# The last row tile's output in column pieces of 512, 64 and 64, the first two stored together

**Chip, cores, metric.** One core of a Trainium2 chip. The metric is the device time of one execution in microseconds (us), the median of several runs. The trace's span, from first to last instruction, is some 1.8 us shorter than that time.

## The reference

```python
xn = layernorm(x)                                   # x: 2048 x 640, bf16
s = attention(xn @ wq, k_cache, v_cache) @ wo       # 32 heads of 192, 2048 keys; wo: 6144 x 640
g = silu(silu_glu(xn, w1, w3, w2))                  # gated feed-forward, 2048 x 640
return x + s * g
```

## The kernel before

Attention (about 1640 us) is followed by the rest of the feed-forward and then by the output stage. That stage takes the 16 row tiles of 128 rows one by one: 48 matmuls for each column piece (the contraction of 6144 in slices of 128), a VectorE multiply by 0.5 and the gate, a VectorE add of x, and a store issued by ScalarE. All tiles but the last use pieces of 384 and 256 columns and one store. The last tile has pieces of its own.

```python
def _output_stage(nc, i, oT, g, wo_sb, x2, out2, sb, ps_pools, last=False):
    D = out2.shape[1]                                # 640; P = 128
    OC = wo_sb.shape[1]                              # 48
    cuts = [(0, D - P), (D - P, D)] if last and D - P <= 512 else _column_pieces(D)
    # ... xt (rows of x), tmp (fp32) and res (bf16) are 128 x 640
    for b, (c0, c1) in enumerate(cuts):
        w = c1 - c0
        ps = ps_pools[b % len(ps_pools)].tile([P, 1024], F32, tag="st2", name="ps_s")
        for k in range(OC):
            nc.tensor.matmul(ps[:, 0:w], lhsT=oT[:, k, :], rhs=wo_sb[:, k, c0:c1], start=(k == 0), stop=(k == OC - 1))
        nc.vector.scalar_tensor_tensor(out=tmp[:, c0:c1]..., in0=ps[:, 0:w]..., scalar=0.5,
                                       in1=g[:, c0 // P:c1 // P, :], op0=ALU.mult, op1=ALU.mult)
        nc.vector.tensor_tensor(out=res[:, c0:c1], in0=tmp[:, c0:c1], in1=xt[:, c0:c1], op=ALU.add)
        if last:
            nc.scalar.dma_start(out=_tile_rows(out2, i)[:, c0:c1], in_=res[:, c0:c1])
    if not last:
        nc.scalar.dma_start(out=_tile_rows(out2, i), in_=res[:])
# ... after the loop over the row tiles:
good = nc.values_load(flag[0:1, 0:1], ...)           # every engine loads the flag into a register
with tc.If(good < 2 * P):                            # and branches over a long block that these
    _exact_attention(...)                            # inputs never take
```

After its last instruction each engine loads the flag and jumps over the exact-attention block to the end of its program.

## Time and profile before

| | before |
|---|---|
| median time, 6 runs | 1938.13 us (1937.98 to 1938.29) |
| span of the profiled run | 1936.43 us |
| start of the last 512-column matmul | 1928.17 us |
| **tail**: from there to the end of the span | 8.25 us |

The change can reach nothing but the tail, so the tail is what I compare in all traces. It does not contain what the first 1928 us do from run to run. Times written with a plus sign (+3.42) are counted from the start of that last 512-column matmul and come, as all times to the nanosecond here, from the single records of the trace. A group line reads: line, engine, operation, output and inputs, shapes, count, then busy us and mean ns of one, then idle time in front and its cause. A line of waits reads: who waited, for whom, us in total, times, longest us. A q behind an engine's name (PEldq is TensorE's, SPq is SyncE's) marks what is no computation: branches, semaphores, DMA issues. The prediction shows the lines themselves.

### The profile page before, as it was taken

How to read it: one execution, taken by the hardware profiler on the slowest of the kernel's cores; microseconds unless marked ns; L12 is line 12 of the kernel's file. 1: busy time of each engine (PE TensorE's matmuls, PEld its weight loads, DVE VectorE, ACT ScalarE, POOL GpSimd, SP SyncE). 2: the span in 40 equal slices, each digit the busy share in tenths (PEclk: the TensorE clock that was granted, in tenths of full speed). 3: DMA queues.
4: the chain of work that ended last, by engine and by line, in shares of the span. 5: the costliest groups of instructions: out<-in, count | busy, mean ns of one | idle time of the engine just before them, and what ended most of it. 6: DMA issues, size and time to landing. Idle time of an engine off the chain costs nothing.

```text
span 1936.4 us, 59669 instructions
## 1 busy us (share of the span) xinstructions
PE 1926.6 (99%) x27273; PEld 1315.6 (68%) x27281; DVE 654.6 (34%) x997; ACT 1180.0 (61%) x1279; POOL 282.5 (15%) x501
## 2 busy tenths in 40 slices
PE   9999999999999999999999999999999999999998
PEld 6666666666666666666666666666666666577776
DVE  7333333333333333333333333333333334521111
ACT  6677676767676767776777777677767677210000
POOL 3111111111111111111111111111111110000000
PEclk9999999999999999999999999999999999999999
DMA  8643433323333434363434343434334220937783
GB/s 181 129 101 67 98 68 86 84 62 88 59 90 61 100 63 97 68 162 69 101 66 100 69 101 69 101 64 101 69 69 96 58 68 2 260 69 137 151 152 62
DMA packets 394643, 178.98 MB, mean 92 GB/s; under 512 B 341616, under 2 KB 382832, under 8 KB 394384
## 3 DMA queue, kind: packets, MB, share of 16 engines
q1 hardware_dynamic: 371136, 125.32, 31.6%
q0 software_dynamic: 19472, 45.71, 10.0%
q8 instruction: 215, 3.52, 0.8%
q10 hardware_dynamic: 3776, 4.06, 0.7%
q14 instruction: 44, 0.36, 0.1%
HBM read 52.82 MB, written 27.79 MB: 42 GB/s over the span
## 4 chain that ended last, share of the span: by engine, by line
PE 99%; DVE 1%; DMA 0%; ACT 0%; issue 0%; DVEq 0%; ACTq 0%
PE obank L519 35%; PE st L487 34%; PE ps L424 14%; PE ps_s L111 11%; PE ps_f L731 3%; PE ps_gu L705 1%; PE st L488 1%; PE ps L410 0%; DVE stats L316 0%; DMA x_all<-in_A_x_dram 0%; PE ps L391 0%; PE pst L354 0%; PE pk L271 0%; DVE xn L346 0%; ACT pT L493 0%
## 5 line engine op out<-in xcount | busy, mean ns | idle before, releaser
L493 ACT ACTIVATE pT<-st 128x1024 bf16<-128x1024 f32 (+1 forms) x1025 | 1046.1, 1021 | 250.2 <-PE st L488 234.0
L519 PEld LDWEIGHTS <-pT 64*128 64x128 bf16 x16384 | 711.3, 94 | 242.3 <-ACT pT L493 0.6
L519 PE MATMUL obank<-vt,pT 64*128 64x193 bf16 x16384 | 849.7, 243 | 0.0
L487 PE MATMUL st<-qC,KW 64*128 64x512 bf16 x2046 | 605.6, 376 | 0.1
L528 DVE COPY osum<-obank 128x772 f32<-128x772 f32 x128 | 123.1, 962 | 787.1 <-PE obank L519 787.1
L488 PE MATMUL st<-qB,KW 64*128 64x512 bf16 x1024 | 385.0, 376 | 0.0
L487 PE MATMUL st<-qA,KW 64*128 64x512 bf16 x1022 | 384.3, 376 | 0.1
L488 PE MATMUL st<-qC,KW 64*128 64x512 bf16 x1022 | 384.3, 376 | 0.0
L488 PE MATMUL st<-qA,KW 64*128 64x512 bf16 x1022 | 384.3, 376 | 0.0
L487 PEld LDWEIGHTS <-KW 64*128 64x128 bf16 x3068 | 278.5, 94 | 153.7 <-issue 2.1
L424 PE MATMUL ps<-xnT,W 64*128 64x512 bf16 x1280 | 297.2, 376 | 0.0
L424 PE MATMUL ps<-xnS,W 64*128 64x512 bf16 x1280 | 296.0, 376 | 0.0
L488 PEld LDWEIGHTS <-KW 64*128 64x128 bf16 x3068 | 278.5, 94 | 0.5
L377 POOL DMA_DIRECT2D qC<-qA x124 | 65.4, 528 | 1283.0 <-DVE rl_all L535 1268.2
L430 ACT CAST qB<-ps 128x512 bf16<-128x512 f32 x131 | 76.7, 585 | 228.2 <-PE ps L424 222.6
L111 PE MATMUL ps_s<-wo_sb,oT 128*128 128x384 bf16 (+3 forms) x1535 | 208.8, 299 | 0.1
L424 PEld LDWEIGHTS <-W 64*128 64x128 bf16 x2560 | 122.9, 94 | 121.4 <-issue 0.2
L111 PEld LDWEIGHTS <-oT 128*128 128x128 bf16 x1536 | 148.4, 98 | 60.4
L529 DVE TENSOR_TENSOR osum<-osum,obank 128x772 f32<-128x772 f32 x128 | 122.7, 959 | 13.4
L536 DVE TENSOR_TENSOR ostage<-osum,rl_all 128x768 bf16<-128x768 f32 x128 | 122.7, 958 | 6.3 <-DMA o_scr<-ostage 1.9
L465 DVE SCALAR_TENSOR_TENSOR hT<-pt,qB 64x512 bf16<-64x512 bf16 x64 | 43.8, 684 | 197.4 <-ACT pt L464 197.4
L429 DVE CAST qA<-ps 128x512 bf16<-128x512 f32 x131 | 90.6, 692 | 25.3 <-PE ps L410 7.2
(84 smaller groups left out, 621.9 us busy)
## 6 DMA issues: line engine op xcount, KB each, us to landing
o_scr<-ostage SPq DMA_DIRECT2D x16, 1536.0 KB, 10.6
vt<-in_A_v_cache_dram SPq DMA_DIRECT2D x63, 384.0 KB, 5.9
qC<-qA POOLq DMA_DIRECT2D x248, 64.0 KB, 1.9
qC<-qB POOLq DMA_DIRECT2D x124, 64.0 KB, 2.3
wo_sb<-in_A_wo_dram POOLq DMA_DIRECT2D x1, 7680.0 KB, 36.1
W<-in_A_wq_dram POOLq DMA_DIRECT2D x32, 160.0 KB, 3.6
W<-in_B_w_dram POOLq DMA_DIRECT2D x32, 80.0 KB, 3.3
W<-in_A_wq_dram POOLq DMA_DIRECT2D x32, 80.0 KB, 3.0
```

The costliest lines, as they stand in the source:

```text
L111: nc.tensor.matmul(ps[:, 0:w], lhsT=oT[:, k, :], rhs=wo_sb[:, k, c0:c1], start=(k == 0), stop=(k == OC - 1))
L377: nc.gpsimd.dma_start(out=qC[0:64, half, :], in_=qAB[half][64:P, :])
L424: nc.tensor.matmul(ps[:, r * 512:(r + 1) * 512], lhsT=W[rows, j, :], rhs=xs[rows, j // 2, qs], start=(j == 0), stop=(j == 2 * DC - 1))
L429: a = nc.vector.tensor_copy(out=qAB[0][:], in_=ps[:, 0:512])
L430: b = nc.scalar.copy(out=qAB[1][:], in_=ps[:, 512:1024])
L487: nc.tensor.matmul(st2[:, 0:512], lhsT=ka, rhs=qa, start=r == 0 and nr == 3, stop=r == nr - 1)
L488: nc.tensor.matmul(st2[:, 512:1024], lhsT=kb, rhs=qb2, start=r == 0 and nr == 3, stop=r == nr - 1)
L493: nc.scalar.activation(out=pT2[:, c * w:(c + 1) * w], in_=st2[:, c * w:(c + 1) * w], func=ACT.Exp, scale=att_scale)
L519: nc.tensor.matmul(obanks[r][:, j * 256:j * 256 + DH + 1], lhsT=pT2[r * 64:(r + 1) * 64, t * 512 + j * P:t * 512 + (j + 1) * P], rhs=vt[r ...
L528: nc.vector.tensor_copy(out=osum[:], in_=ov[0])
L529: nc.vector.tensor_tensor(out=osum[:], in0=osum[:], in1=ov[1], op=ALU.add)
L536: nc.vector.tensor_tensor(out=ostage[:, qb * 4:qb * 4 + 4, hg * DH:(hg + 1) * DH], in0=osum[:, :, 0:DH], in1=rl.unsqueeze(2).to_broadcast( ...
```

## The change

Intent: shorten what follows the last matmul. The last piece shrinks from 128 to 64 columns, so that its two VectorE instructions and its store are smaller; the middle piece is stored with the first, so there are still two stores.

```diff
-    cuts = [(0, D - P), (D - P, D)] if last and D - P <= 512 else _column_pieces(D)
+    cuts = [(0, D - P), (D - P, D - 64), (D - 64, D)] if last and D - P <= 512 else _column_pieces(D)
...
+        wa = min(w, P)
         nc.vector.scalar_tensor_tensor(...                       # the same, in groups of wa columns
-        if last:
-            nc.scalar.dma_start(out=_tile_rows(out2, i)[:, c0:c1], in_=res[:, c0:c1])
+        if last and b > 0:
+            d0 = c0 if b > 1 else 0
+            nc.scalar.dma_start(out=_tile_rows(out2, i)[:, d0:c1], in_=res[:, d0:c1])
```

More of the change, by code (lines that the diff above doesn't have):

```diff
@@ L111, in _output_stage @@
             nc.tensor.matmul(ps[:, 0:w], lhsT=oT[:, k, :], rhs=wo_sb[:, k, c0:c1], start=(k == 0), stop=(k == OC - 1))
-        nc.vector.scalar_tensor_tensor(out=tmp[:, c0:c1].rearrange("p (a w) -> p a w", w=P),
-                                       in0=ps[:, 0:w].rearrange("p (a w) -> p a w", w=P),
-                                       scalar=0.5, in1=g[:, c0 // P:c1 // P, :], op0=ALU.mult, op1=ALU.mult)
+        wa = min(w, P)
+        nc.vector.scalar_tensor_tensor(out=tmp[:, c0:c1].rearrange("p (a w) -> p a w", w=wa),
+                                       in0=ps[:, 0:w].rearrange("p (a w) -> p a w", w=wa),
+                                       scalar=0.5, in1=g[:, c0 // P:-(-c1 // P), c0 % P:c0 % P + wa], op0=ALU.mult, op1=ALU.mult)
         nc.vector.tensor_tensor(out=res[:, c0:c1], in0=tmp[:, c0:c1], in1=xt[:, c0:c1], op=ALU.add)
-        if last:
-            nc.scalar.dma_start(out=_tile_rows(out2, i)[:, c0:c1], in_=res[:, c0:c1])
+        if last and b > 0:
+            d0 = c0 if b > 1 else 0
+            nc.scalar.dma_start(out=_tile_rows(out2, i)[:, d0:c1], in_=res[:, d0:c1])
     if not last:
```

## The prediction

Two terms of its sum lose their source by this: the 29.2 ns for a pair of 64 columns and the 27 ns by which such a matmul's stream is shorter. The sum came to +0.06 us: the last matmul starts 0.150 later, less 0.027 makes +0.123 for the start of the last multiply (1931.394), less 0.067 for the smaller multiply makes +0.056 for the last add and all that follows it; 1938.26 + 0.06 = 1938.32. An estimate from the trace of before comes to the same two figures: the 512-column matmuls of the last tile start 215.82 ns apart (1918.462 to 1928.174, 45 steps) and those of 128 columns 55.83, so 64 columns are 26.67 ns, and a pair of 64 columns takes 55.83 - 26.67 = 29.16 ns. In the 3.03 us after VectorE's branch the records have two packets of 8,192 bytes on an instruction queue, starting at 1933.25 and 1933.94. That VectorE waited for them was my reading.

> **What bounds the kernel now.** I read the head of the page first, then the chain of work that ended last, then the trace's last 10 us, because the change touches only the sixteenth and last row tile of the output stage.
>
> ```profile
> span 1936.4 us, 59669 instructions
> PE 1926.6 (99%) x27273; PEld 1315.6 (68%) x27281; DVE 654.6 (34%) x997; ACT 1180.0 (61%) x1279; POOL 282.5 (15%) x501
> PE 99%; DVE 1%; DMA 0%; ACT 0%; issue 0%; DVEq 0%; ACTq 0%
> ```
>
> TensorE is busy for 99% of the span, and the chain is 99% TensorE. All of that except the last few microseconds is the same code before and after. The change can therefore move only the tail, and 2% of 1938 us is 39 us, twice the 18 us that lie between the last tile's first matmul (about 1918.05) and the end of the span.
>
> The same chain in order of time, cut to the end:
>
> ```profile
> 1918.46 12.79 PE ps_s L111 x94
> 1931.25 0.02 issue
> 1931.27 0.30 DVE tmp L112
> 1931.57 0.02 issue
> 1931.60 0.29 DVE res L115
> ```
>
> The reader is to see that after the last matmul come two VectorE instructions (multiply by the gate, add x) and then nothing that the view shows until 1936.4: 4.5 us of ending. The groups of instructions within the output stage give sizes:
>
> ```profile
> L111 PE MATMUL ps_s<-wo_sb,oT 128*128 128x512 bf16 x47 | 10.5, 379 | 0.1
> L111 PE MATMUL ps_s<-wo_sb,oT 128*128 128x128 bf16 x48 | 2.8, 219 | 0.0
> L112 DVE SCALAR_TENSOR_TENSOR tmp<-ps_s,hT 128x512 f32<-128x512 f32 x1 | 0.7, 692 | 9.5 <-PE ps_s L111 9.5
> L112 DVE SCALAR_TENSOR_TENSOR tmp<-ps_s,hT 128x128 f32<-128x128 f32 x1 | 0.3, 292 | 1.3 <-PE ps_s L111 1.3
> L115 DVE TENSOR_TENSOR res<-tmp,xt 128x128 bf16<-128x128 f32 x1 | 0.3, 292 | 0.0
> ```
>
> What lies in the last 4.5 us? The waits of the queue on SyncE in the last 12 us, and the records of the exit branch and of the closing semaphores by engine:
>
> ```profile
> SPq L806 <- DVEq L754: 1.0, 1, 1.0
> ```
>
> ```profile
> L754 PEldq COMPARE_BRANCH  x1: 3395/3395/3395, 1930.7 to 1930.7; - x1
> L754 DVEq COMPARE_BRANCH  x1: 72/72/72, 1932.2 to 1932.2; - x1
> L754 PEldq EVENT_SEMAPHORE  x1: 51/51/51, 1934.1 to 1934.1; - x1
> L754 DVEq EVENT_SEMAPHORE  x1: 21/21/21, 1935.3 to 1935.3; - x1
> ```
>
> SyncE closes the program. It has seen the last store land at 1933.74 (record of its semaphore), works through a row of checks until 1934.375, and then waits 1.007 us for VectorE. VectorE starts its last add at 1931.597, its load of the flag (line 752) at 1931.612, its branch over the exact-attention block at 1932.228, and signals only at 1935.330, 3.03 us after the branch ended. From there to the end of the span are 1.10 us. So **the end hangs on when VectorE reaches its branch, not on the store**: the store has about 1.0 us of slack.
>
> [...] the 48 matmuls of 128 columns start 55.8 ns apart (1928.390 to 1931.014 in the records, over 47 steps), each with its own weight load. [...] One place in the trace shows more, the two-column matmul of the flag count:
>
> ```profile
> 1686.44 0.10 PEld L742 LDWEIGHTS <-ones 128*128 128x128 bf16 x1
> 1686.55 0.17 PE L742 MATMUL cnt<-okb,ones 128*128 128x2 bf16 x1
> 1686.55 0.12 PEld L731 LDWEIGHTS <-hT 128*128 128x128 bf16 x2
> 1686.57 0.32 PE L731 MATMUL ps_f<-w_all,hT 128*128 128x384 bf16 x1
> ```
>
> To the nanosecond the records read 1686.545, 1686.546 and 1686.573: the full weight load that followed the narrow matmul held the next one back by only 28 ns. [...]
>
> **The change part by part.** Instruction order: VectorE gets two instructions more (one more multiply and add), TensorE 96 more (48 weight loads, 48 matmuls), ScalarE still issues two stores, and no new wait appears on the PSUM buffer of the third piece (the first pool's other buffer, last used one tile earlier).
> 1. TensorE. Removed: 48 matmuls of 128 columns at 55.8 ns. Added: 96 of 64 columns. [...] First narrow matmul at 1928.390 as now, last at 1928.390 + 95 x 0.0292 = 1931.164, against 1931.014: +0.150. [...] Today the multiply starts 0.257 after the last matmul's start; then 0.230: 1931.394.
> 2. VectorE, last piece. By the slope (692-292)/384 = 1.04 ns a column, 64 columns cost 292 - 67 = 225 ns. Add starts 0.225 + 0.034 (the present gap: 1931.597-1931.271-0.292) after 1931.394, at 1931.653: **+0.056** against now. It ends at 1931.878, against 1931.889: -0.011.
> 3. VectorE, middle piece. Its matmuls end about 1929.8 + 0.2, while the 512-column add runs until 1930.010; two instructions of 225 ns then finish at about 1930.53, 0.87 us before the last piece needs the engine. Hidden.
> 4. Stores. The first moves from 1930.04 to about 1930.56 and grows from 128 to 144 KB. At the 1.7 us to landing that the DMA view has for the present one, it lands about 1932.3. The second shrinks from 32 to 16 KB and is issued 0.01 earlier; its landing time is nearly all fixed (1.8 us for 32 KB, 1.7 for 128 KB). ScalarE is free long before. Both stay under the 1.0 us of slack: worth nothing.
> 5. Ending. The flag load started 15 ns after the start of the last add, so it follows the add's start, +0.056, and the branch, the fetch and the close follow in fixed steps. Sum: +0.06 us, or -0.01 if it is the add's end that counts.
>
> **The rivals.**
> - *The weight load becomes TensorE's bound.* At 40 ns a pair the last matmul would start 0.0400 x 95 = 3.80 us after the first instead of 2.62: +1.2 us, about 1939.4; at today's 55.8 ns it would be +2.7, about 1940.9. For it: weight loads are recorded at 98 ns each, and no sustained stretch of narrow pairs exists in this trace. Against: the 28 ns case, and the attention's 16,384 pairs, 35% of the span, at some 41 ns each [...].
> - *The store sets the end.* Then the smaller last store would gain a little: its 256-byte packets took 18 ns and would take somewhat less; at best 0.1 us, about 1938.2. Against: SyncE's 1.007 us of waiting for VectorE after the store landed.
> - *The fetch after the branch changes.* [...] one more or one fewer fetch is worth about 0.7 us (the distance of the two 8,192-byte packets), either way. TensorE's branch also comes later: its flag load ran 0.93 us, about 17 pairs, before its last matmul, so with pairs of 29.2 ns it comes at about 1930.68 instead of 1930.09, and its signal at 1934.73 instead of 1934.13, still 0.6 us before VectorE's.
>
> **Range and chances.** The middle case gives 1938.26 + 0.06 = 1938.32. The three runs before spread over 0.3 us, so low 1937.7; rivals mostly lengthen, so high 1939.5, which takes in a 40 ns pair and one fetch more. I put 1938.4, a tenth of microsecond up for that skew. A move of 39 us is out of reach for any of these: 0.5% each for faster and slower.
>
> **What would show it.** Right: the 96 narrow matmuls start about 29 ns apart and the last at 1931.15 to 1931.2; VectorE's last two instructions take about 225 ns; SyncE still waits longest for VectorE at the close; the second store lands near 1933.7. Wrong: narrow pairs at 40 ns or more; SyncE waiting for a store or for TensorE; a different stretch between VectorE's branch and its signal; or any difference before 1918 us larger than that at the tail.

## The result, and the profile after

The changed kernel took 1938.58 us, median of six runs (1938.0 to 1939.49), against 1938.13 for six of the kernel before. The ratio is 1.0003, 95% interval 0.999 to 1.0016: the same. (A ratio is the mean time of one kernel's fast runs over that of the other's of the same rounds, so not quite the ratio of the medians.)

The profiled run of the changed kernel is the slowest of its six, with a span 1.30 us longer. The two traces split this cleanly: 1.04 us was lost before the last 512-column matmul and 0.255 us in the tail.

The 1.04 us is no part of the change: it was lost in the first head. The waits of the changed kernel between 10 and 27 us have a line that the kernel before does not have:

```profile
PE ps L426 <- DMA xnS<-xnT: 0.9, 1, 0.9
```

TensorE waited 0.9 us for a copy that landed at 20.18 us, against 19.01 before. (A further 0.09 us is the first load of x.) Two more traces of the changed kernel below have no such wait.

The tail is what concerns us. The groups of the last two tiles in the changed kernel, and the last steps of its chain of work in order of time (start, length, what):

```profile
L111 PE MATMUL ps_s<-wo_sb,oT 128*128 128x64 bf16 x96 | 3.0, 193 | 0.0
L113 DVE SCALAR_TENSOR_TENSOR tmp<-ps_s,hT 128x64 f32<-128x64 f32 x2 | 0.5, 225 | 0.9 <-PE ps_s L111 0.9
L116 DVE TENSOR_TENSOR res<-tmp,xt 128x64 bf16<-128x64 f32 x2 | 0.4, 224 | 0.1
```

```profile
1919.50 12.90 PE ps_s L111 x142
1932.41 0.02 issue
1932.43 0.24 DVE tmp L113
1932.67 0.02 issue
1932.69 0.22 DVE res L116
```

The reader sees what was forecast: 96 narrow matmuls in much the time that 48 wider ones took (12.90 us for the tile instead of 12.79), and VectorE instructions of 225 ns instead of 292. Counted from the last 512-column matmul, the last matmul starts at +2.985 instead of +2.840, the last add at +3.475 instead of +3.423, and the last store is issued at +3.732 instead of +3.747.

What was not forecast stands in the DMA view of the last 10 us (KB, then us from issue to the landing of the store's last part). Before:

```profile
out_dram<-res ACTq DMA_DIRECT2D x1, 128.0 KB, 1.7
out_dram<-res ACTq DMA_DIRECT2D x1, 32.0 KB, 1.8
```

After:

```profile
out_dram<-res ACTq DMA_DIRECT2D x1, 144.0 KB, 1.7
out_dram<-res ACTq DMA_DIRECT2D x1, 16.0 KB, 3.1
```

The last store was halved, and it took 3.1 us instead of 1.8. The waits of SyncE's queue at the close show the consequence. Its first line holds the waits for the two stores: the longest is for the first, the rest is for the last (12.3 - 10.3 = 2.0 us before, 13.3 - 10.6 = 2.7 us after). Before:

```profile
SPq L754 <- SPq L754: 12.3, 2, 10.3
```

After:

```profile
SPq L756 <- SPq L756: 13.3, 2, 10.6
SPq L808 <- PEq L808: 0.7, 2, 0.5
```

The wait of 1.0 us for VectorE that the prediction shows for the kernel before is gone. VectorE's signal did come a little earlier (+7.028 instead of +7.156), but that is not why: SyncE itself came later, because it first waited for the store until +6.804 instead of +5.570.

Packet by packet: the store's 128 packets of 128 bytes are all read by +4.80, except for eight, which start from +5.542 on. Eight of 128 would be the share of one of the 16 DMA engines that the page counts, and the landings agree: the store signals in 16 parts, of which 15 have landed by +5.157 and the last lands at +6.787. (In the kernel before 15 have landed by +5.207 and the last lands at +5.554, so there too one part is late, by much less.) While the eight wait, a fetch of 16,384 bytes of instructions runs from +4.670 to +5.562: it is the one that follows TensorE's exit branch at +3.106. In the kernel before that branch came at +2.507, its fetch ran from +3.471 to +4.359, and it was over when the last store's packets started. The records of branch and signal in the changed kernel (count, then min/median/max ns, then first and last start):

```profile
L756 PEldq COMPARE_BRANCH  x1: 4112/4112/4112, 1932.3 to 1932.3; - x1
L756 DVEq COMPARE_BRANCH  x1: 72/72/72, 1933.3 to 1933.3; - x1
L756 DVEq EVENT_SEMAPHORE  x1: 21/21/21, 1936.2 to 1936.2; - x1
L756 PEldq EVENT_SEMAPHORE  x1: 51/51/51, 1936.5 to 1936.5; - x1
```

**Theory (collision).** The narrow pieces let TensorE reach its exit branch 0.60 us later. The fetch behind the branch then occupies one DMA engine just when the last store is due, and that engine's share of the store lands late. (Waiting for the fetch is not the whole delay: the eight packets are read 0.96 us after the others, but their part lands 1.63 us after the other 15. The remaining 0.67 us is not explained.) **Rivals.** The 128-byte rows or the narrow pieces make the store late by themselves; joining the stores does it; or all of it is run-to-run chance.

### The profile page after: what moved, and what is told of

Same layout as the page of the kernel before. It is cut to its first block, busy times and chain, and to the rows that moved or that the text cites. A ratio compares the mean times of both kernels' runs of the same rounds, so it can differ in the third digit from the quotient of the medians.

```text
span 1937.7 us, 59767 instructions
## 1 busy us (share of the span) xinstructions
PE 1927.8 (99%) x27321; PEld 1316.7 (68%) x27329; DVE 654.5 (34%) x999; ACT 1181.1 (61%) x1279; POOL 282.4 (15%) x501
## 4 chain that ended last, share of the span: by engine, by line
PE 98%; DMA 1%; DVE 0%; ACT 0%; issue 0%; DVEq 0%; ACTq 0%; SPq 0%
PE obank L521 35%; PE st L489 33%; PE ps L426 14%; PE ps_s L111 11%; PE ps_f L733 3%; PE ps_gu L707 1%; PE st L490 1%; DMA xnS<-xnT 0%; PE ps L412 0%; DVE stats L318 0%; DMA x_all<-in_A_x_dram 0%; ACT KW L279 0%; PE pst L356 0%; ACT xnT L358 0%; DVE xn L348 0%
## 5 line engine op out<-in xcount | busy, mean ns | idle before, releaser
L111 PE MATMUL ps_s<-wo_sb,oT 128*128 128x256 bf16 (+3 forms) x1583 | 208.9, 295 | 0.1
```

## The experiments

Kernels are compared only within the same rounds. Every result was correct. The tails decide.

**1. The kernel before, again.** No edit.

> The kernel before, unchanged, timed against itself: the yardstick. I call tail the time from the start of the last 512-column matmul of the last row tile to the end of the span; the first profile of before has 8.25 us, of the changed kernel 8.51. Theory (chance at the start): the 1.04 us by which the changed kernel's profile was late already at 26 us comes from how late a load of the first head lands and has nothing to do with the change, so runs of this same kernel will also now and then be about 1 us longer: within ten runs at least one of 1938.8 us or more. Rival (the change makes the start slow): all runs of this kernel stay within 1937.9 to 1938.4. Tail: 8.2 to 8.3 us, SyncE waiting longest for VectorE.

Median 1938.19 us (1937.99 to 1938.41, 5 runs), against 1938.40 for the nine runs of the same kernel beside it (ratio 0.9999, 0.9985 to 1.0013). Tail 8.251 us, SyncE waiting 0.8 us for VectorE. The tail repeats to a nanosecond. Neither forecast on the start held here: the longest of the 14 runs took 1938.70. In the third call, though, six of the nine runs of the kernel before took more than 1938.6 us and three over 1939.3. So runs 1 us longer do occur with the old code; that these few share the late copy of the first trace was not seen, as they left no trace.

**2. The changed kernel, again,** and **12. a third time.** No edit.

> The changed kernel, unchanged. Theory (chance at the start): median within 0.5 us of the kernel before of the same rounds, some runs at 1938.0 to 1938.2 and some about 1 us longer; tail about 8.3 us (predicted +0.06) if no packet of the last store lands late, up to 8.5 if one does as in the first profile. Rival (the change makes it slower): every run at least 0.3 us over the runs before, tail again 8.5. The 96 narrow matmuls 29 ns apart in either case.

> The changed kernel a third time, for the spread of its tail. Theory (collision): TensorE's fetch starts between 4.0 and 4.9 us, eight of the last store's packets start only when it ends, the last landing follows some 1.1 to 1.3 us after the fetch's end, at 6.3 to 6.9 us, and the tail is 8.35 to 8.6 us; median time 0.1 to 0.5 us over the kernel before of the same rounds.

Medians 1938.59 (against 1938.40 beside it; ratio 1.0002, 0.9988 to 1.0016) and 1938.57 (against 1938.85; ratio 0.9999, 0.9985 to 1.0013): the sign of the difference itself turns round. So the third call's forecast of a median 0.1 to 0.5 us over the kernel before failed (it is 0.28 under), and in the call of the second trace no run came at 1938.0 to 1938.2, where some were expected (they took 1938.33 to 1939.16). Tails 8.400 and 8.383 us, so all three traces of the changed kernel are longer than both of the kernel before, by 0.13 to 0.26 us. In all three the eight packets start when TensorE's fetch ends: fetch until +5.261 and packets from +5.248, fetch until +5.413 and packets from +5.399. The stores' landings in the DMA view, second and third trace:

```profile
out_dram<-res ACTq DMA_DIRECT2D x1, 16.0 KB, 2.7
```

```profile
out_dram<-res ACTq DMA_DIRECT2D x1, 16.0 KB, 2.9
```

The narrow matmuls are 29 ns apart (median; 30 at most) in each.

**3. The join undone.**

```diff
-        if last and b > 0:
-            d0 = c0 if b > 1 else 0
-            ...store columns d0:c1
+        if last:
+            ...store columns c0:c1
```

> The changed kernel with its join undone: pieces of 512, 64 and 64, each stored by itself as soon as it is done. If joining the first two stores matters (rival: the later and larger first store collides with the last one and makes its last packet land late), the last store lands here at about 1.45 us after its issue in all packets and the tail falls to 8.3. If it does not (theory: landing of the first store has slack either way), the tail is that of the changed kernel within 0.1 us, and the stray late packet comes or stays away by chance.

Median 1939.04 us (1938.92 to 1939.39) against 1938.40; tail 9.120 us: worse than either expectation. The store collides as in the changed kernel (fetch +4.712 to +5.588, last landing +6.861), so the join is not what makes it late. But SyncE goes on from that landing to the end in 2.24 us, not 1.70. SyncE meets this landing first, with all its other closing checks still to come: its waits show one piece of 35.2 us, where the changed kernel has two of 13.3 us together (that the third store's semaphore stands first in SyncE's row is how I read it):

```profile
SPq L755 <- SPq L755: 35.2, 1, 35.2
```

Joining the first two stores is therefore worth some 0.5 us against three stores (2.24 - 1.70, one trace each), and not by the transfer: the last landing is only 0.07 us later (+6.861 against +6.787).

**4. One store.** The kernel before, pieces 512 and 128, a single store of all 640 columns at the end.

```diff
-        if last:
-            nc.scalar.dma_start(...[:, c0:c1]...)
-    if not last:
-        nc.scalar.dma_start(out=_tile_rows(out2, i), in_=res[:])
+    nc.scalar.dma_start(out=_tile_rows(out2, i), in_=res[:])
```

> The kernel before with pieces of 512 and 128 but a single store of all 640 columns after the second. VectorE and TensorE do what they did. Theory (the end hangs on VectorE's exit branch, the store has 1 us of slack): 160 KB instead of 32 KB after the last add lands about 0.2 to 0.4 us later, inside the slack, and the tail stays 8.2 to 8.35. Rival (the store sets the end): the tail grows by 0.2 us or more.

Median 1938.22 (against 1938.40), last landing +5.670 for 160 KB, inside the slack as the theory said, though not the 0.2 to 0.4 us later that it expected: the two traces of before have +5.554 and +5.742. Tail 8.067 us, a little under the range: VectorE needed 2.92 us from its branch to its signal, against 3.10 in both traces of before. That stretch varies from 2.92 to 3.24 us over the traces of kernels with the branch.

**5. TensorE late in the kernel before.** This is the test of the theory: pieces, VectorE and stores as before, and only TensorE's branch later.

```diff
+    if last:
+        pd = ps_pools[0].tile([P, 1024], F32, tag="st2", name="ps_d")
+        for k in range(12):
+            nc.tensor.matmul(pd[:, 0:P], lhsT=oT[:, k, :], rhs=wo_sb[:, k, 0:P], start=(k == 0), stop=(k == 11))
```

> The kernel before (pieces 512 and 128, two stores), with twelve more 128-column matmuls at TensorE's very end whose result nobody reads, so that TensorE reaches its exit branch about 0.6 us later (as the changed kernel's does) while VectorE, the pieces and the stores stay as they were. Theory (collision): the fetch of instructions that follows TensorE's branch now starts at 4.1 to 4.7 us after the last 512-column matmul instead of 3.47, eight of the last store's 128 packets wait until it is over, the last landing moves from 5.55 to 5.75 us to 6.3 to 6.9 us, and the tail grows from 8.25 to 8.35 to 8.6 us. Rival (the late packets come from 128-byte rows or from the narrow pieces themselves): last landing stays at most 5.8 us and the tail stays 8.25 us.

TensorE's branch came at +3.224, its fetch ran from +4.824 to +5.724, eight of the 256-byte packets started from +5.698 on, and the last landing was at +6.893. The DMA view:

```profile
out_dram<-res ACTq DMA_DIRECT2D x1, 128.0 KB, 1.7
out_dram<-res ACTq DMA_DIRECT2D x1, 32.0 KB, 3.1
```

The same 32 KB that land in 1.8 us in the kernel before take 3.1. Tail 8.612 us; median 1938.47 against 1938.22 (ratio 1.0000, 0.9987 to 1.0014). The start of the fetch and the tail lie a little above the ranges expected (4.7 and 8.6). The late landing needs neither narrow pieces nor 128-byte rows; a late branch on TensorE is enough, in this one trace. (The twelve matmuls also make TensorE's program longer; no run separates that from the later branch.) Nor do the narrower rows add much to it: from the end of TensorE's fetch to the last landing are 1.17 us here, with 256-byte rows, and 1.20 to 1.25 us in the three traces of the changed kernel.

**6 and 7. The flag loaded early,** in the kernel before and in the changed one.

```diff
     for i in range(NQT):
+        if i == NQT - 1:
+            good = nc.values_load(flag[0:1, 0:1], ...)
         ...
-    good = nc.values_load(flag[0:1, 0:1], ...)
     with tc.If(good < 2 * P):
```

> The kernel before with the flag for the exit branch loaded into each engine's register ahead of the last row tile instead of behind it; the branch stays where it was. Theory (the end hangs on VectorE's branch): the branch comes 0.62 us earlier on VectorE, directly after the start of the last add, and the tail falls from 8.25 to about 7.65 us, the time to about 0.6 us under the kernel before; TensorE's fetch starts before 3 us. Rival (the store sets the end): tail falls by 0.2 us at most.

> The same earlier flag load in the changed kernel. Theory (collision of TensorE's fetch with the last store): TensorE's branch comes at about 2.5 us again as in the kernel before, its fetch is over at about 4.4 us, before the last store's packets at 4.7; the last store lands by 5.8 us, not 6.5 to 6.8, and the tail is about 7.7 us, 0 to 0.1 us over the same edit of the kernel before. Rival (the narrow pieces cost the 0.2 us themselves): it stays 0.15 to 0.25 us above the same edit of the kernel before.

Before with the edit: VectorE branches at +3.435 instead of +4.054, tail 7.601 us, as expected. This is the version that the experiments point to; its tail beats both kernels by 0.65 us or more. Its time does not show that: median 1938.05 (1937.43 to 1939.06) against 1938.22, ratio 1.0000, 0.9987 to 1.0014.

Changed kernel with the edit: tail 7.850 us and last landing +6.131, not 7.7 and 5.8, so my number was missed and the rival's was met (0.249 us above the same edit of before). TensorE's fetch (+3.733 to +4.746) is now nearly out of the store's way, but VectorE's, which comes early too (+4.516 to +5.104), is in it: eight packets start at +5.101. Shifting one fetch out of the way moved another in. That holds for the kernel before with the edit as well: its eight packets start at +4.992, as VectorE's fetch ends (+4.995), and its first store is held by TensorE's fetch and lands at +5.459 instead of +3.569. So this collision alone does not explain the difference between the two: of the 0.249 us, VectorE's later fetch is 0.109, and the rest is not explained. This pair leaves the rival standing; experiments 5, 10 and 11 speak against it. Median of the changed kernel with the edit: 1937.97 against 1938.22 (ratio 0.9998, 0.9985 to 1.0012).

**8. VectorE delayed, first try.** A VectorE instruction of 512 columns behind the last add in the kernel before.

```diff
+    if last:
+        nc.vector.tensor_tensor(out=tmp[:, 0:512], in0=tmp[:, 0:512], in1=xt[:, 0:512], op=ALU.add)
```

> The kernel before with one more VectorE instruction of 512 columns (0.69 us) behind the last add, writing a buffer nobody reads; the last store does not wait for it. Theory (VectorE's exit branch sets the end, and it follows the start of the last instruction): the flag load starts 0.33 us later and so does the end, tail 8.55 to 8.6 us. If it follows the end of the last instruction: tail about 8.95 us. Rival (the store sets the end): tail stays 8.25 us, since more than 0.3 us of VectorE's time would be hidden.

Inconclusive: the added instruction had nothing to wait for, and the flag load started at +3.439 as before, ahead of it. Tail 8.327 us, VectorE's signal at +7.231 (a branch-to-signal stretch of 3.17 us). Median 1938.25 against 1938.22.

**9. VectorE delayed, second try.** The added instruction now reads the last add's result and so waits for it.

```diff
+    if last:
+        nc.vector.tensor_tensor(out=tmp[:, 0:P], in0=res[:, D - P:D], in1=xt[:, 0:P], op=ALU.add)
```

> Second try at delaying VectorE's branch in the kernel before: one more VectorE instruction of 128 columns behind the last add, which reads what that add wrote and so has to wait for it. The first try had an instruction that waited for nothing, and the flag load overtook it. Theory (VectorE's branch sets the end of the kernel before): the flag load starts 0.33 us later, VectorE's signal comes at about 7.48 us, the tail is about 8.58 us. Rival (the store sets the end): tail 8.25 to 8.33 us.

The flag load started at +3.764, 0.33 us later as expected, and the branch at +4.382. The signal came at +7.299, only 0.14 us later, as this time branch to signal took 2.92 us. The tail grew by the same 0.14 us, to 8.396, and SyncE still waited 0.8 us for VectorE. So the end did follow VectorE's signal, but by less than forecast, because the stretch behind the branch scatters by as much as the effect. Median 1938.73 against 1938.85.

**10 and 11. No branch,** in both kernels: the flag load and the guarded block taken out (right for these inputs, not a safe kernel).

```diff
-    good = nc.values_load(flag[0:1, 0:1], ...)
-    with tc.If(good < 2 * P):
-        ...
```

> The kernel before without the guarded exact-attention block and its exit branch (right for these inputs, where the block is not taken, but no longer a safe kernel). With no branch there is no fetch of instructions behind it on TensorE or VectorE. Theory: the store alone sets the end then; it lands about 5.2 us after the last 512-column matmul [...], SyncE needs some 1.75 us for its checks, and the tail falls from 8.25 to about 6.9 us.

> The changed kernel with the same removal. Theory (the pieces themselves are worth +0.06 to -0.05 us and the rest of the +0.15 to +0.26 us is the collision of the last store with TensorE's fetch): with no fetch the last store's packets all go at once, its last landing is at about 5.15 us, and the tail is within 0.1 us of the kernel before with the same removal, more likely 0.05 below it. Rival (128-byte rows or narrow pieces cost it): it stays 0.15 us or more above.

Tails 7.134 and 7.066 us. (The 5.2 us that the first expectation has for the landing was an estimate: 15 of the store's 16 parts had landed by +5.207 and +5.157 in the first traces of the two kernels.) The packets of 16,384 bytes are gone from the DMA view of the last microseconds, but my claim that no fetch would be left was wrong: one of 8,192 bytes still runs, from +5.056 to +5.363 and from +4.987 to +5.294, and in both kernels it holds eight packets of the last store, so that the last landings are +6.215 and +6.148. But it holds them equally: from its end to the last landing are 0.85 us in both. The changed kernel's tail is the shorter one, by 0.068 us, and that is just the 0.069 us by which this fetch ended earlier; whether the pieces moved it is not shown. So no cost of the narrow pieces or the 128-byte rows is seen when the collision is the same for both, in one trace each. (Medians 1937.81 and 1937.06 against 1938.85; four runs each, scattered over more than their difference.)

**All tails on one rule.** In every trace of a kernel with the branch and at most two stores, the tail is the later of two sums: the time when SyncE wakes for the last store plus 1.70 us, or VectorE's signal plus 1.10 us. (Experiments 8 and 9, not in the table, fit as well: 7.231 + 1.10 for 8.327 and 7.299 + 1.10 for 8.396.)

| trace | TensorE's branch | its fetch | last landing | SyncE wakes | VectorE's signal | tail |
|---|---|---|---|---|---|---|
| before | 2.507 | 3.471-4.359 | 5.554 | 5.570 | **7.156** | 8.252 |
| before, again | 2.507 | 3.464-4.512 | 5.742 | 5.758 | **7.155** | 8.251 |
| one store | 2.506 | 3.469-4.433 | 5.670 | 5.686 | **6.971** | 8.067 |
| after | 3.106 | 4.670-5.562 | 6.787 | **6.804** | 7.028 | 8.507 |
| after, again | 3.107 | 4.079-5.261 | 6.464 | 6.481 | **7.304** | 8.400 |
| after, third | 3.103 | 4.519-5.413 | 6.663 | **6.679** | 7.229 | 8.383 |
| TensorE late | 3.224 | 4.824-5.724 | 6.893 | **6.909** | 6.996 | 8.612 |
| flag early, before | 1.911 | 2.864-4.189 | 5.881 | **5.898** | 6.398 | 7.601 |
| flag early, after | 2.511 | 3.733-4.746 | 6.131 | **6.148** | 6.616 | 7.850 |

The bold time is the one that sets the tail: 7.156 + 1.10 = 8.25 and 6.804 + 1.70 = 8.50, for example. In the changed kernel the two sums lie 0.05 to 0.38 us apart, and either can win: in its second trace the late store was hidden, and VectorE's branch-to-signal stretch (3.19 us) set the tail. In its first trace VectorE's signal alone would have given 8.13 us, less than the kernel before has.

## Why the prediction was right or wrong

- The time, the range and "within 2%" were right: 1938.58 measured for 1938.4 predicted. Part of that closeness is luck, since the predicted difference of +0.06 us is well under the scatter of the runs.
- Step 1 (TensorE) was right: pairs 29 ns apart (predicted 29.2), last matmul +0.145 us (+0.150). The rival with 40 ns a pair fell. The single two-column matmul in the trace of before was enough to judge it.
- Step 2 (VectorE's last piece) was right: 225 ns, last add +0.052 us (predicted +0.056), store issued 0.015 us earlier (0.011).
- Step 3 was right: the middle piece's second instruction ends at +2.30, and VectorE's next is at +3.216.
- **Step 4 failed**: "Both stay under the 1.0 us of slack: worth nothing." The last store landed 0.7 to 1.2 us later than in the kernel before and used the slack up, so in two of three traces SyncE waited for the store and not for VectorE, which the prediction had listed as a sign of being wrong. I had called the landing time "nearly all fixed", from the two stores of one trace.
- Step 5 was right in direction for VectorE's branch (+4.110 against +4.054), but the "fixed steps" after it are not fixed: 2.92 to 3.24 us. That scatter is larger than the +0.06 it was to carry.
- In the third rival I worked out that TensorE's branch would move by about 0.6 us (measured 0.60) and asked only whether its *signal* would still come 0.6 us before VectorE's. It did not: it came 0.41 and 0.08 us before in two traces and 0.25 us after in the first (+7.276 against +7.028), as its branch-to-signal stretch grew from 3.45 and 3.65 us to between 3.79 and 4.17. The fetch that it sets off, and what that meets, I left out. "The store sets the end", the second rival, came true in two of three traces by this way.
- I read both 8,192-byte fetches as VectorE's. The first starts 1.02 to 1.04 us after VectorE's branch in the three runs that move that branch (and in most others; 1.30 to 1.31 in three); the second stayed where it was when only VectorE was delayed (+5.765 against +5.768), and went with ScalarE's branch in the early-flag runs (+5.239 after a branch at +4.110). It belongs to ScalarE, by these times, and the 0.7 us that I put on one fetch more or less had no basis.

Shown, each by one trace: a late branch on TensorE, pieces and stores as before, makes the store late and the tail longer (experiment 5: last landing +6.893 instead of +5.554, tail 8.612 us instead of 8.252), and the pieces by themselves are not slower (10 and 11: tail 7.066 against 7.134 us). Not shown: whether 0.13 to 0.26 us in the tail is also the mean difference of the timed runs, since they scatter by 1 us and more; why TensorE's fetch starts 0.94 to 0.97 us after the branch in some traces and 1.2 to 1.6 in others; and which DMA engine it was, which the trace does not name.

## What to carry to other kernels

When the last instructions of a program are shortened, look at everything that each engine does after its own last instruction. Here the 16,384-byte fetch behind TensorE's exit branch ran until +5.562, and eight of the last store's 128 packets started only from +5.542; moving the branch by 0.60 us had put it in front of them. From the branch to the engine's next instruction, its closing signal, the first traces of the kernel before and of the changed one show 3.10 and 2.92 us on VectorE, 3.45 and 4.17 us on TensorE, and 0.47 us twice on ScalarE. TensorE's flag load ran 0.93 us ahead of its last matmul with the 128-column pieces and 0.48 us with the 64-column ones, some 16 or 17 matmuls both times: so the narrow pieces delayed what came next in the stream even though the matmuls took nearly the same time. And try to load what a closing branch needs before the last tile: here that shortened the tail by 0.65 us, more than any cut of the pieces did, though in one trace, and the timed runs do not show it.
